# A second place for the sum of halves, rows' columns interleaved, a table loaded and cast later, and the last mixed sums of the first sequence in two halves

## The chip, the cores and the metric

One core of one Trainium2 chip runs the whole program in one launch. The metric is the device time in microseconds (us), the median of three runs. The traces come from one profiled execution of each kernel. Engines are named as the profile names them: PE (TensorE), DVE (VectorE), ACT (ScalarE), POOL (GpSimd), SP (SyncE, which here issues all loads and stores). Each engine works through its own instructions in a fixed order.

## The reference

There are eight sequences of 3136 rows with 256 columns. First a spectral layer, then a block with a two-dimensional transform and an MLP:

```
X  = rfft(x, axis=1);  Yr = Xr@w_r - Xi@w_i + b_r;  Yi = Xr@w_i + Xi@w_r + b_i
Y  = soft_threshold(Yr, 0.01) + 1j*soft_threshold(Yi, 0.01);  y = irfft(Y, n=3136)
u  = y + real(fft(fft(y, axis=1), axis=2))
un = (u - mean(u)) / sqrt(var(u) + 1e-6)
out = u + relu(un @ w_ch1) @ w_ch2
```

The weights are real-valued matrices of 256x256 (spectral) and 256x1024, 1024x256 (MLP).

## The kernel before

**Stages.** Transforms over 3136 are done as 64 x 49 with tables. For each sequence `b` there are ten generators: `p1` (64-point transform, result to DRAM in `aq` or `ad`), `p2_f2` (49-point transform of `af`, a load of that result, with the table `tff`), `p2_w` (weights, bias, threshold, giving `Y`), `p2_mix` (the two-dimensional transform's real part from `Y`, as sums and differences `mq`, stored to `md`), `p2_yt` and `p2_g2` (inverse 49-point transform with the table `tif`, result `bev` stored to `bd`), `p3_norm` (load `bf` from `bd` and `mt` from `md`, inverse 64-point transform, `ut` = the sum of both, row statistics and the scale `rs`), `p3_tr` (transposes of `ut`), `p3_mlp1` and `p3_mlp2`. Stages `p2_*` work in four quarters `q` of the frequencies, stages `p3_*` in 6 or 7 groups of up to 4 blocks of 128 rows (`z` blocks; 52 groups in all).

**Two numbers for one.** Most products are made with a high part and a rest, three matmuls each (`mm3`, L166): `uth` and `utl`, `hh` and `hl`, `tih` and `til`. The first sequence's transforms use plain fp32 instead.

**The order.** Every generator yields a due time (multiples of `T`, with shares like `TR`, `MLAG`, `NRM`) ahead of each step; a heap runs the steps by due time, and that is the priority with which the scheduler places the instructions on each engine at build time. `tc.issue_after(x)` and `behind(key, ...)` place an instruction behind another on the same engine. A tile is a named place (`tag`) with `bufs` copies: an instruction that writes a new tile waits until the last user of the place that it takes over is done.

**What the change touches.** `rows_f2` (L441) loads `af` into three places. In `p2_mix` (L557) the four products of a quarter come first and are then combined in one go (L608 to L616): on DVE for the first sequence, on POOL for the others, with copies on ACT; then the stores to `md` (L621 to L635). In `p2_yt` the table `tif` is loaded and for b > 0 cast to `tih` on ACT (L658), its rest `til` taken on DVE. In `p3_norm` the scales of a group are stored to a small DRAM tile `rd` (L737) as rows of 128. In `p3_tr` each pair of blocks, as soon as its `ut` is there, is transposed into one PSUM bank for both column halves `k` (L779), and evicted to `uth` (ACT, L781) and `utl` (DVE). `p3_mlp1` ends with the adds on POOL that form `total` from `uth` and `utl` (L806), in the one place `tot`:

```
total = sb.tile([128, 2, 512], F32, tag="tot", bufs=1, name="total")
...
gp.tensor_add(total[:, k, cols], uth[:, k, cols].bitcast(F32), utl[:, k, cols].bitcast(F32))
```

`p3_mlp2` loads the scales, spread over all partitions, as `rb` (L824) at step 1 of its 8, multiplies the result by it (L830), adds `total` (L833) and stores the sum from the `total` tile to the output (L834). `uth` and `utl` have two places each; a group's are free when its first MLP matrix and the adds of `total` are done. `ut` has four places. `split_double` uses `tot` once, early, for a part of the weights.

Of the kernel before, what the change touches and what calls it, by code (L numbers as in the profile page):

```python
# [20 lines left out]
D = 256  # L21
# [119 lines left out]
def spectral_block(ctx: ExitStack, tc: tile.TileContext, x, w_ri, b_ri, w1, w2,  # L141
# [30 lines left out]
    def split_double(name, h, l, parts, centred):  # L172
# [11 lines left out]
        if spare:  # L184
            pair = sb.tile([128, 2, 512], F32R, tag="tot", bufs=1, name="cv_pair")
        for sl, raw in parts:
# [240 lines left out]
    def clock2(b, q):  # L427
# [3 lines left out]
        return t0 + step * q, step, f2w, w0, ww, w0 + ww  # L431
    xt, yt_, tabs = {}, {}, {}

# [7 lines left out]
    def rows_f2(b, q, s):  # L441

        u0 = 8 * q
        af = sb.tile([98, 4 * D], F32, tag="af", bufs=3, name="af")
        ad, u = a_dram[b](u0 + 4 * s)
        ld = nc.sync.dma_start(out=af.rearrange("p (u d) -> p u d", d=D), in_=ad.rearrange("n r c u d -> (n r c) u d")[:98, u:u + 4])
        tff = sb.tile([98, 4, 100], F32, tag="tff", bufs=3, name="tff")
        nc.sync.dma_start(out=tff, in_=c_tf[:, u0 + 4 * s:u0 + 4 * s + 4, :])
        if b == 0:
            af_ld[2 * q + s] = ld.ins  # L450
            done.add(("af", 2 * q + s))
        return af, tff
# [53 lines left out]
    def p2_w(b):  # L506

        for q in range(4):
# [19 lines left out]
            for o in range(2):  # L528
                yield base + STEP * WW * o / 2
                gw = prod("wr", o, xs_[len(xs_) // 2:])  # L530
                ks = sb.tile([128, 8, S], F32, tag="ks", bufs=2, name="ks")
                sc.copy(ks, gw)
                for c in range(2):
# [12 lines left out]
    def p2_mix(b):  # L546
# [12 lines left out]
        for q in range(4):  # L559
# [24 lines left out]
            mq = sb.tile([100, 2, 4, 2, 128], F32, tag="mq", bufs=2, name="mq")  # L584
            even, odd = mq[:, 1, :, 0], mq[:, 1, :, 1]
            for ui in range(4):
# [19 lines left out]
                va.tensor_add(mq[:, 0, ui, 1, 0:1], gv[:, 0, 1, 0:1], odd[:, ui, 0:1])  # L606

            for i, f in ((0, va.tensor_add), (1, va.tensor_sub)):  # L608
                f(even[:, :, i::2], even[:, :, i::2], odd[:, :, 0:1].to_broadcast((100, 4, 64)))
            eng = gp if b else va  # L610
            eng.tensor_add(mq[:, 0, :, 0, 1:], even[:, :, 1:], odd[:, :, 1:])
            eng.tensor_sub(mq[:, 0, :, 1, 1:], even[:, :, 1:], odd[:, :, 1:])
            sc.copy(mq[:, 0, :, 0, 0:1], even[:, :, 0:1])
            sc.copy(even[:, :, 1:], mq[:, 0, :, 1, 1:])
            (va.tensor_copy if b else sc.copy)(odd[:, :, 1:], mq[:, 0, :, 0, 1:])
            sc.copy(odd[:, :, 0:1], mq[:, 0, :, 1, 0:1])  # L616
            mr = mq.rearrange("p a u h e -> p a (u h e)")
# [22 lines left out]
    def p2_yt(b):  # L640

        for q in range(4):
# [4 lines left out]
            for i in range(4):  # L647
                yield base + STEP * (M0 + 0.022 + 0.185 * i)
                s = i // 2
                if i % 2 == 0:  # L650
                    tif = sb.tile([100, 4, 98], F32, tag="tif", bufs=2, name="tif")
                    behind(3 if b or q else 1, out=tif, in_=c_ti[:, u0 + 4 * s:u0 + 4 * s + 4, :])
                    if b == 0:
                        tabs[b, q, s] = tif, None
                    else:
                        tih = sb.tile([100, 4, 98], F32R, tag="tih", bufs=1, name="tih")
                        til = sb.tile([100, 4, 98], F32R, tag="til", bufs=1, name="til")
                        sc.copy(tih, tif)  # L658
                        lo_v(til, tif, tih)
# [18 lines left out]
    def p2_g2(b):  # L678

        bd = b_dram[b] = dr.tile([NM, 2, 2, U, D], F32, tag="bd", bufs=4, name=f"bd{b}")  # L680
        for q in range(4):
            base, STEP, F2W, W0, WW, M0 = clock2(b, q)
            for i in range(4):
# [13 lines left out]
                u = 8 * q + 2 * i  # L697
                st_eng.dma_start(out=bd.rearrange("n r c u d -> (n r c) u d")[:98, u:u + 2], in_=bev.rearrange("p (u d) -> p u d", d=D))
        done.add(("b", b))
# [9 lines left out]
    def p3_norm(b):  # L709

        def finish(m, n, g, mt):
# [23 lines left out]
            if m + n == g0 + z:  # L735
                rd = scales[b, gi] = dr.tile([512], F32, tag="rd", bufs=4, name="rd")
                st_eng.dma_start(out=rd[:128 * z].rearrange("(j p) -> p j", j=z), in_=rall[:, :z].rearrange("p j o -> p (j o)"))  # L737
        for m, n in [(4 * i, 4) for i in range(6)] + [(NM - 1, 1)] * (b % 2):
# [26 lines left out]
    def p3_tr(b):  # L765
        for gi, (g0, z) in enumerate(GROUPS[b % 2]):
            t0, T3 = clock3(b, g0)
            for i, n in parts_of[z]:
                yield t0 + T3 * (TR + i / 4)
                if i == 0:  # L770
                    uth = sb.tile([128, 2, 512], F32R, tag="uth", bufs=UTHB, name="uth")
                    utl = sb.tile([128, 2, 512], F32R, tag="utl", bufs=2, name="utl")
                    uthl[b, gi] = uth, utl
                ut = uts.pop((b, g0 + i))
                g = gtile("g_ut")
                gv = g.rearrange("p (k t) -> p k t", k=2)
                for j in range(n):
                    for k in range(2):
                        te.transpose(gv[:, k, j * 128:(j + 1) * 128], ut[:, j, k * 128:(k + 1) * 128], ident)  # L779
                tw = slice(i * 128, i * 128 + n * 128)  # L780
                sc.copy(uth[:, :, tw], gv[:, :, :n * 128])  # L781
                lo_v(utl[:, :, tw], gv[:, :, :n * 128], uth[:, :, tw])

    def p3_mlp1(b):
        for gi, (g0, z) in enumerate(GROUPS[b % 2]):
# [15 lines left out]
            yield t0 + T3 * 1.0  # L801
            total = sb.tile([128, 2, 512], F32, tag="tot", bufs=1, name="total")
            for k in range(2):
# [5 lines left out]
    def p3_mlp2(b):  # L809
        for gi, (g0, z) in enumerate(GROUPS[b % 2]):  # L810
            t0, T3 = clock3(b, g0)
            w = z * 128
            for f in range(8):
# [5 lines left out]
                for k, o in enumerate(ops):  # L819
                    es = slice(k * 128, k * 128 + 128)  # L820
                    mm3(o, w2h[:, f, es], w2l[:, f, es], hh[:, :w], hl[:, :w], start=f == 0, stop=f == 7, first=1)
                if f == 1:
                    rb = sb.tile([128, 512], F32, tag="rb", bufs=1, name="rb")
# [107 lines left out]
```

## Time and profile before

| | before |
|---|---|
| median of 3 runs | 1941.72 us (1937.23 to 1942.70) |
| profiled execution | 1940.12 us, of which 1938.3 us from the first to the last instruction (span) |
| mean granted TensorE clock | 0.973 |
| busy: PE, DVE, ACT, POOL | 1841.4, 1192.2, 807.5, 560.4 us |

Busy time is the union of an engine's instructions. The granted clock is a share of 2.4 GHz; it has two levels, 0.5 (1.2 GHz) and 1, and a value between is a mean over the stretch. Line numbers (L806) are those of the kernel before.

### The profile page before, as it was taken

How to read it: one execution, taken by the hardware profiler on the slowest of the kernel's cores; microseconds unless marked ns; L12 is line 12 of the kernel's file. 1: busy time of each engine (PE TensorE's matmuls, PEld its weight loads, DVE VectorE, ACT ScalarE, POOL GpSimd, SP SyncE). 2: the span in 40 equal slices, each digit the busy share in tenths (PEclk: the TensorE clock that was granted, in tenths of full speed). 3: DMA queues.
4: the chain of work that ended last, by engine and by line, in shares of the span. 5: the costliest groups of instructions: out<-in, count | busy, mean ns of one | idle time of the engine just before them, and what ended most of it. 6: DMA issues, size and time to landing. Idle time of an engine off the chain costs nothing.

```text
span 1938.3 us, 29340 instructions
## 1 busy us (share of the span) xinstructions
PE 1841.4 (95%) x10044; PEld 1504.3 (78%) x10044; DVE 1192.2 (62%) x2603; ACT 807.5 (42%) x1864; POOL 560.4 (29%) x1028
## 2 busy tenths in 40 slices
PE   7886999899999999999999999999999999989998
PEld 4565787688787888877788788887878888867788
DVE  3664766566565766666666566656656656645543
ACT  2563544344444434444343444444444444322222
POOL 0003333222333422323323243332233433212121
PEclk8997999999999999999999999999999999999999
DMA  8763866455535756476444765546543543336211
GB/s 249 221 201 108 191 158 128 114 140 128 148 91 123 168 117 145 76 184 144 99 116 118 163 154 115 105 123 165 130 133 81 143 99 85 75 86 112 62 37 33
DMA packets 176365, 245.59 MB, mean 127 GB/s; under 512 B 42640, under 2 KB 123608, under 8 KB 175960
## 3 DMA queue, kind: packets, MB, share of 16 engines
q1 hardware_dynamic: 176216, 243.72, 52.3%
q8 instruction: 79, 1.29, 0.4%
q14 instruction: 70, 0.57, 0.1%
HBM read 140.79 MB, written 102.86 MB: 126 GB/s over the span
## 4 chain that ended last, share of the span: by engine, by line
PE 74%; DMA 12%; DVE 6%; POOL 3%; SPq 2%; issue 2%; ACT 2%; DVEq 0%; POOLq 0%; ACTq 0%
PE h L166 23%; PE o L166 23%; PE g_w L166 7%; PE g_f L477 4%; PE g_g L166 3%; DMA out_dram<-total 3%; PE g_g L377 2%; PE g_yt L665 2%; DMA mt<-md 2%; DMA bd<-bev 2%; PE g_ut L779 2%; PE g_f L377 2%; DMA xf<-in_x 2%; DMA md<-mq 1%; POOL total L806 1%
## 5 line engine op out<-in xcount | busy, mean ns | idle before, releaser
L799 DVE SCALAR_TENSOR_TENSOR hl<-h,hh 128x512 fp32r<-128x512 f32 (+2 forms) x416 | 273.1, 657 | 382.2 <-ACT hh L798 375.9
L798 ACT ACTIVATE hh<-h 128x512 fp32r<-128x512 f32 (+2 forms) x416 | 238.5, 574 | 417.3 <-PE h L166 396.5
L166 PE MATMUL o<-hl,w2h 128*128 128x512 f32 (+2 forms) x832 | 333.8, 401 | 9.9 <-DVE hl L799 7.6
L166 PE MATMUL h<-utl,w1h 128*128 128x512 f32 (+2 forms) x832 | 325.6, 391 | 2.8 <-DVE utl L156 2.8
L166 PE MATMUL h<-uth,w1l 128*128 128x512 f32 (+2 forms) x832 | 320.8, 386 | 0.0
L166 PE MATMUL h<-uth,w1h 128*128 128x512 f32 (+2 forms) x832 | 319.4, 384 | 0.0
L166 PE MATMUL o<-hh,w2l 128*128 128x512 f32 (+2 forms) x832 | 318.5, 383 | 0.0
L166 PE MATMUL o<-hh,w2h 128*128 128x512 f32 (+2 forms) x832 | 318.3, 383 | 0.0
L806 POOL TENSOR_TENSOR total<-uth,utl 128x256 f32<-128x256 f32 x200 | 146.4, 763 | 527.0 <-DMA out_dram<-total 404.2
L166 PEld LDWEIGHTS o<-hl,w2h 128*128 128x128 f32 x832 | 158.3, 190 | 47.1 <-DVE hl L799 13.5
L166 PEld LDWEIGHTS h<-utl,w1h 128*128 128x128 f32 x832 | 158.1, 190 | 35.8 <-issue 6.5
L166 PEld LDWEIGHTS h<-uth,w1l 128*128 128x128 f32 x832 | 158.2, 190 | 33.9 <-issue 4.1
L166 PEld LDWEIGHTS o<-hh,w2l 128*128 128x128 f32 x832 | 158.0, 190 | 29.7 <-issue 0.8
L166 PEld LDWEIGHTS h<-uth,w1h 128*128 128x128 f32 x832 | 158.3, 190 | 25.7
L166 PEld LDWEIGHTS o<-hh,w2h 128*128 128x128 f32 x832 | 158.6, 191 | 19.6
L477 PEld LDWEIGHTS g_f<-tff,af 98*128 98x128 f32 x1024 | 141.9, 200 | 32.5 <-DVE wdl L156 9.9
L477 PE MATMUL g_f<-tff,af 98*128 98x100 f32 x1024 | 150.3, 282 | 11.5 <-DMA af<-aq 9.1
L159 POOL TENSOR_TENSOR Xl<-xx,Xh 128x400 fp32r<-128x400 f32 x84 | 91.2, 1087 | 192.2 <-ACT Xh L494 188.9
L696 ACT COPY bev<-g_g 98x512 f32<-98x512 f32 x128 | 74.8, 585 | 113.9 <-PE g_g L166 59.2
L537 DVE SCALAR_TENSOR_TENSOR y<-g_w,bias,ks 128x400 f32<-128x400 f32 x128 | 80.5, 629 | 49.4 <-PE g_w L166 34.0
L540 POOL TENSOR_TENSOR Y<-y,m 128x400 f32<-128x400 f32 x56 | 62.5, 1117 | 166.5 <-DVE m L539 160.0
L665 PE MATMUL g_yt<-ident,Y 128*100 128x128 f32 x512 | 85.1, 281 | 24.5 <-POOL Y L544 7.8
(156 smaller groups left out, 3271.8 us busy)
## 6 DMA issues: line engine op xcount, KB each, us to landing
bd<-bev SPq DMA_DIRECT2D x128, 196.0 KB
bf<-bd SPq DMA_DIRECT2D x96, 256.0 KB
mt<-md SPq DMA_DIRECT2D x192, 128.0 KB
out_dram<-total SPq DMA_DIRECT2D x88, 256.0 KB
af<-ad SPq DMA_DIRECT2D x56, 392.0 KB
md<-mq SPq DMA_DIRECT2D x112, 192.0 KB
ad<-ev SPq DMA_DIRECT2D x84, 256.0 KB
xf<-in_x SPq DMA_DIRECT2D x39, 512.0 KB
```

What stands on the lines that cost most here:

```text
L159: gp.tensor_sub(out_, full, hi.bitcast(F32))
L166: te.matmul(o, l, r, start=start and i == 0, stop=stop and i == 2)
L377: return te.matmul(banks[i][64 * j:64 * j + 64], mat[rows, rows], movs[i][j], start=True, stop=True)
L477: te.matmul(gf[:, k, :, s], afs[s][:, ui * D + k * 128:ui * D + k * 128 + 128], tfs[s][:, ui].rearrange("p (c j) -> p c j", c=2), start=Tr ...
L537: va.scalar_tensor_tensor(y1, gw, bias[:, c, o:o + 1], ks, op0=ALU.add, op1=ALU.add)
L540: (va if b == 0 or o == 0 else gp).tensor_sub(y[:, o, :, c, :], y1, m)
L665: te.transpose(gt[:100, (v * 2 + o) * 128:(v * 2 + o + 1) * 128], y[:, o, place].rearrange("p c j -> p (c j)"), ident)
L696: sc.copy(bev, g[:98])
L779: te.transpose(gv[:, k, j * 128:(j + 1) * 128], ut[:, j, k * 128:(k + 1) * 128], ident)
L798: sc.activation(hh[:, :w], h[:, :w], AF.Relu)
L799: va.scalar_tensor_tensor(hl[:, :w], h[:, :w], 0.0, hh[:, :w].bitcast(F32), op0=ALU.max, op1=ALU.subtract)
L806: gp.tensor_add(total[:, k, cols], uth[:, k, cols].bitcast(F32), utl[:, k, cols].bitcast(F32))
```

## The change

There are six edits. (1) The place `tot` has two copies; `af` has two copies instead of three, and every third `af` of the first sequence takes `tot`. (2) In the last quarter of the first sequence the mixed sums are combined after every two of four blocks. (3) For the first quarter of the second sequence the table `tif` is loaded behind the last store to `bd`; for b > 0 the cast to `tih` stands behind the last copy `ks` of its quarter. (4) A group's columns stand in row order: row p of block j is column p*z + j, so that the scales are stored as 128 short rows of z numbers, the transposes write with a step of z, and the host reads the output back in that order. (5) `p3_tr` transposes all blocks of a group for column half 0, then for half 1, each into one bank. (6) `rb` is loaded at step 4 of 8.

```diff
@@ split_double, spectral_block, rows_f2 @@
-            pair = sb.tile([128, 2, 512], F32R, tag="tot", bufs=1, name="cv_pair")
+            pair = sb.tile([128, 2, 512], F32R, tag="tot", bufs=2, name="cv_pair")
...
-    xt, yt_, tabs = {}, {}, {}
+    xt, yt_, tabs, ks_in = {}, {}, {}, {}
...
-        af = sb.tile([98, 4 * D], F32, tag="af", bufs=3, name="af")
+        tag = "tot" if b == 0 and (2 * q + s) % 3 == 2 else "af"
+        af = sb.tile([98, 4 * D], F32, tag=tag, bufs=2, name="af")
@@ p2_w, p2_mix @@
-                sc.copy(ks, gw)
+                ks_in[b, q] = sc.copy(ks, gw).ins
...
-            even, odd = mq[:, 1, :, 0], mq[:, 1, :, 1]
+            odd = mq[:, 1, :, 1]
+
+            def combine(us):
+
+                even, odd = mq[:, 1, us, 0], mq[:, 1, us, 1]
+                for i, f in ((0, va.tensor_add), (1, va.tensor_sub)):
+                    f(even[:, :, i::2], even[:, :, i::2], odd[:, :, 0:1].to_broadcast((100, us.stop - us.start, 64)))
+                eng = gp if b else va
+                eng.tensor_add(mq[:, 0, us, 0, 1:], even[:, :, 1:], odd[:, :, 1:])
+                eng.tensor_sub(mq[:, 0, us, 1, 1:], even[:, :, 1:], odd[:, :, 1:])
+                sc.copy(mq[:, 0, us, 0, 0:1], even[:, :, 0:1])
+                sc.copy(even[:, :, 1:], mq[:, 0, us, 1, 1:])
+                (va.tensor_copy if b else sc.copy)(odd[:, :, 1:], mq[:, 0, us, 0, 1:])
+                sc.copy(odd[:, :, 0:1], mq[:, 0, us, 1, 0:1])
+            halves = b == 0 and q == 3
             for ui in range(4):
...
                 va.tensor_add(mq[:, 0, ui, 1, 0:1], gv[:, 0, 1, 0:1], odd[:, ui, 0:1])
-
-            for i, f in ((0, va.tensor_add), (1, va.tensor_sub)):
...
-            sc.copy(odd[:, :, 0:1], mq[:, 0, :, 1, 0:1])
+                if halves and ui % 2:
+                    combine(slice(ui - 1, ui + 1))
+            if not halves:
+                combine(slice(0, 4))
@@ p2_yt, p2_g2 @@
-                    behind(3 if b or q else 1, out=tif, in_=c_ti[:, u0 + 4 * s:u0 + 4 * s + 4, :])
+                    behind("bd" if b == 1 and q == 0 else 3 if b or q else 1, out=tif, in_=c_ti[:, u0 + 4 * s:u0 + 4 * s + 4, :])
...
-                        sc.copy(tih, tif)
+                        with tc.issue_after(ks_in[b, q]):
+                            sc.copy(tih, tif)
...
-                st_eng.dma_start(out=bd.rearrange("n r c u d -> (n r c) u d")[:98, u:u + 2], in_=bev.rearrange("p (u d) -> p u d", d=D))
+                stored = st_eng.dma_start(out=bd.rearrange("n r c u d -> (n r c) u d")[:98, u:u + 2], in_=bev.rearrange("p (u d) -> p u d", d=D))
+        af_ld["bd"] = stored.ins
         done.add(("b", b))
@@ p3_norm, p3_tr @@
-                st_eng.dma_start(out=rd[:128 * z].rearrange("(j p) -> p j", j=z), in_=rall[:, :z].rearrange("p j o -> p (j o)"))
+                st_eng.dma_start(out=rd[:128 * z].rearrange("(p j) -> p j", j=z), in_=rall[:, :z].rearrange("p j o -> p (j o)"))
...
-            for i, n in parts_of[z]:
-                yield t0 + T3 * (TR + i / 4)
-                if i == 0:
+            w = z * 128
+            for k in range(2):
+                yield t0 + T3 * (TR + k / 4)
+                if k == 0:
...
-                ut = uts.pop((b, g0 + i))
+                    blocks = [(uts[b, g0 + i], j) for i, n in parts_of[z] for j in range(n)]
                 g = gtile("g_ut")
-                gv = g.rearrange("p (k t) -> p k t", k=2)
-                for j in range(n):
-                    for k in range(2):
-                        te.transpose(gv[:, k, j * 128:(j + 1) * 128], ut[:, j, k * 128:(k + 1) * 128], ident)
-                tw = slice(i * 128, i * 128 + n * 128)
-                sc.copy(uth[:, :, tw], gv[:, :, :n * 128])
-                lo_v(utl[:, :, tw], gv[:, :, :n * 128], uth[:, :, tw])
+                gv = g[:, :w].rearrange("p (t j) -> p j t", j=z)
+                for i, (ut, j) in enumerate(blocks):
+                    te.transpose(gv[:, i], ut[:, j, k * 128:(k + 1) * 128], ident)
+                sc.copy(uth[:, k, :w], g[:, :w])
+                lo_v(utl[:, k, :w], g[:, :w], uth[:, k, :w])
@@ p3_mlp1, p3_mlp2 @@
-            total = sb.tile([128, 2, 512], F32, tag="tot", bufs=1, name="total")
+            total = sb.tile([128, 2, 512], F32, tag="tot", bufs=2, name="total")
...
-                if f == 1:
+                if f == 4:
                     rb = sb.tile([128, 512], F32, tag="rb", bufs=1, name="rb")
```

On POOL, in the second sequence's second quarter (`y_1718` and `y_1766` before, `y_1724` and `y_1779` after, are the two subtractions L540 that make its `Y`; `vv`, `rs` the norm of a group). Before:

```order
L732 TENSOR_SCALAR vv<-vv 128x2
L733 TENSOR_TENSOR rs<-rs,vv 128x2
L540 TENSOR_TENSOR Y<-y_1718,m 128x8x50
L540 TENSOR_TENSOR Y<-y_1766,m 128x8x50
L159 TENSOR_TENSOR Xl<-xx,Xh 128x4x100
```

After:

```order
L743 TENSOR_SCALAR vv<-vv 128x2
L744 TENSOR_TENSOR rs<-rs,vv 128x2
L816 TENSOR_TENSOR total<-uth,utl 128x256 x2
L541 TENSOR_TENSOR Y<-y_1724,m 128x8x50
L816 TENSOR_TENSOR total<-uth,utl 128x256 x2
L541 TENSOR_TENSOR Y<-y_1779,m 128x8x50
L159 TENSOR_TENSOR Xl<-xx,Xh 128x4x100
```

The four adds of the second group now stand around these subtractions; before, they came twenty rows later, ahead of the next quarter's.

On SP, at the end of the first sequence's sums (`md` stores, `bf` and `mt` loads of its first norm groups). Before:

```order
L748 DMA bf<-bd_87 128x2x256 x2
L282 DMA tif<-c_ti 100x392
L621 DMA md_86<-mq 24x2x1024
L622 DMA md_86<-mq 2x1x1024
L623 DMA md_86<-mq 24x2x1024
L633 DMA md_86<-mq 24x2x1024
L634 DMA md_86<-mq 2x1x1024
L635 DMA md_86<-mq 24x2x1024
L446 DMA af<-ad_85 98x1024
L448 DMA tff<-c_tf 98x400
L748 DMA bf<-bd_87 128x2x256 x2
L753 DMA mt<-md_86 32x4x256
```

After:

```order
L449 DMA tff<-c_tf 98x400
L630 DMA md_86<-mq 24x2x1024
L631 DMA md_86<-mq 2x1x1024
L632 DMA md_86<-mq 24x2x1024
L642 DMA md_86<-mq 24x2x1024
L643 DMA md_86<-mq 2x1x1024
L644 DMA md_86<-mq 24x2x1024
L759 DMA bf<-bd_87 128x2x256 x2
L449 DMA tff<-c_tf 98x400
L764 DMA mt<-md_86 32x4x256
```

The second `bf` pair and the `tif` load now follow the `md` stores, and only two pairs instead of three stand ahead of the first `mt` load.

On PE, between the first two sets of transposes (`g_w`, `g_f`, `g_yt` belong to the second sequence, `h` is the first MLP product). Before:

```order
L166 MATMUL g_w<-Xh,wdl 128x400
L665 MATMUL g_yt<-ident,Y 100x128
L477 MATMUL g_f_1398<-tff,af 128x2x50 x4
L477 MATMUL g_f_1411<-tff,af 128x2x50 x4
L665 MATMUL g_yt<-ident,Y 100x128
L477 MATMUL g_f_1433<-tff,af 128x2x50 x4
L779 MATMUL g_ut<-ident,ut 128x128 x4
L166 MATMUL h<-utl,w1h 128x512
```

After:

```order
L166 MATMUL g_w<-Xh,wdl 128x400
L166 MATMUL h<-utl,w1h 128x512
L166 MATMUL h<-uth,w1h 128x512
L166 MATMUL h<-uth,w1l 128x512
L166 MATMUL h<-utl,w1h 128x512
L166 MATMUL h<-uth,w1h 128x512
L166 MATMUL h<-uth,w1l 128x512
L675 MATMUL g_yt<-ident,Y 100x128
L790 MATMUL g_ut<-ident,ut 128x128 x4
```

Six matmuls of `h`, those of column half 0, now stand ahead of the second four transposes.

## Rows read from the trace of the kernel before

**Rows 1.** The page: busy time of PE (share of the span, instructions) and the engines behind it, the packets of all DMA queues, and the chain that ended last by engine.

```profile
PE 1841.4 (95%) x10044; PEld 1504.3 (78%) x10044; DVE 1192.2 (62%) x2603; ACT 807.5 (42%) x1864; POOL 560.4 (29%) x1028
DMA packets 176365, 245.59 MB, mean 127 GB/s; under 512 B 42640, under 2 KB 123608, under 8 KB 175960
PE 74%; DMA 12%; DVE 6%; POOL 3%; SPq 2%; issue 2%; ACT 2%; DVEq 0%; POOLq 0%; ACTq 0%
```

**Rows 2.** Busy time by stretches: start:end and length in us, then for PE, PEld, DVE, ACT and POOL the busy us and (x) the instructions, the granted clock, the share that the DMA engines were busy, GB/s.

```profile
0.00:128.00 128.00, 105.87 (x456) 66.35 (x456) 75.72 (x170) 55.67 (x121) 0.41 (x6) 0.91 0.75 230
128.00:182.00 54.00, 34.09 (x178) 28.57 (x177) 23.87 (x56) 23.53 (x57) 18.40 (x27) 0.78 0.54 153
155.00:160.00 5.00, 1.48 (x9) 1.15 (x7) 1.17 (x3) 0.49 (x1) 0.00 (x0) 0.92 1.00 256
328.00:341.00 13.00, 8.37 (x39) 7.14 (x38) 4.75 (x11) 5.09 (x11) 5.51 (x8) 0.74 0.62 194
369.00:382.00 13.00, 5.55 (x26) 4.65 (x25) 2.51 (x6) 3.38 (x8) 3.52 (x6) 0.74 0.93 293
950.00:960.00 10.00, 7.46 (x32) 5.46 (x32) 5.35 (x7) 4.13 (x10) 6.30 (x8) 0.83 0.32 110
1406.00:1416.00 10.00, 7.89 (x44) 5.74 (x36) 4.56 (x6) 2.55 (x6) 6.36 (x7) 0.83 0.12 41
1558.00:1570.00 12.00, 7.77 (x48) 7.52 (x47) 5.86 (x15) 3.53 (x12) 6.65 (x6) 0.72 0.17 47
```

**Rows 3.** The line L806 by itself: the adds' durations in ns (least, median, most) with the first and last start in us, and one of the releasers for which POOL sat idle before them (us, times).

```profile
L806 POOL TENSOR_TENSOR total<-uth,utl x200: 450/745/1213, 168.3 to 1924.5; 128x256 f32<-128x256 f32 x100
  DMA out_dram<-total: 404.2, 38
```

**Rows 4.** Timeline of PE in eight stretches: start and duration in us, instruction, count, and in brackets the idle time before it and what ended it.

```profile
335.31 0.51 PE L166 MATMUL g_g<-yl,tih 100*98 100x256 f32 x1 [4.63 <-DVE Xl L156]
378.06 0.88 PE L665 MATMUL g_yt<-ident,Y 128*100 128x128 f32 x3 [7.45 <-POOL Y L544]
492.06 0.53 PE L665 MATMUL g_yt<-ident,Y 128*100 128x128 f32 x3 [2.41 <-POOL Y L540]
843.62 0.50 PE L166 MATMUL o<-hl,w2h 128*128 128x512 f32 x1 [1.26 <-DVE hl L799]
953.38 0.53 PE L665 MATMUL g_yt<-ident,Y 128*100 128x128 f32 x3 [2.46 <-POOL Y L540]
1304.37 0.50 PE L166 MATMUL o<-hl,w2h 128*128 128x512 f32 x1 [1.17 <-DVE hl L799]
1411.00 0.53 PE L665 MATMUL g_yt<-ident,Y 128*100 128x128 f32 x3 [2.10 <-POOL Y L540]
1564.01 0.58 PE L166 MATMUL o<-hl,w2h 128*128 128x256 f32 x1 [4.23 <-DVE hl L799]
```

**Rows 5.** The chain of work that ended last, in order of time, of the whole execution: start, duration, what. Five of its longest pieces.

```profile
318.25 11.52 DMA out_dram<-total
369.53 5.54 DMA out_dram<-total
604.37 12.87 DMA xf<-in_x
831.92 4.92 DMA rb<-rd
865.84 11.56 DMA bd<-bev
```

**Rows 6.** Timeline from 95 to 180 us of DVE, ACT, SP (SPq: the issue alone) and PE, columns as in rows 4.

```profile
143.69 1.51 DVE L612 TENSOR_TENSOR mq<-mq 100x508 f32<-100x508 f32 x1
145.24 0.61 ACT L614 COPY mq<-mq 100x508 f32<-100x508 f32 x1 [0.34 <-DVE mq L612]
145.87 0.89 SPq L748 DMA_DIRECT2D bf<-bd  x2
147.30 0.54 SPq L621 DMA_DIRECT2D md<-mq  x1
164.88 1.29 DVE L714 TENSOR_TENSOR ut<-g_g,mt 128x512 f32<-128x512 f32 x2 [8.68 <-DMA mt<-md]
165.72 1.09 PE L779 MATMUL g_ut<-ident,ut 128*128 128x128 f32 x4 [9.24 <-DVE ut L714]
176.36 0.80 PE L166 MATMUL h<-utl,w1h 128*128 128x512 f32 x1 [2.81 <-DVE utl L156]
```

**Rows 7.** Groups by line and shape: count, busy us, mean ns of one, idle us before them.

```profile
L779 PE MATMUL g_ut<-ident,ut 128*128 128x128 f32 x392 | 61.1, 279 | 10.4 <-DVE ut L714 10.4
```

**Rows 8.** Timeline of PE from 1012 us, at the full clock: one set of transposes and the matmuls of `o` behind it.

```profile
1013.00 0.60 PE L779 MATMUL g_ut<-ident,ut 128*128 128x128 f32 x4
1013.67 0.39 PE L166 MATMUL o<-hh,w2h 128*128 128x512 f32 x1
1013.90 0.39 PE L166 MATMUL o<-hh,w2l 128*128 128x512 f32 x1
```

**Rows 9.** Timeline of SP and PE: a load of `af`, and its first reader's matmuls.

```profile
792.71 0.33 SPq L446 DMA_DIRECT2D af<-ad  x1
833.10 1.48 PE L477 MATMUL g_f<-tff,af 98*128 98x100 f32 x12
```

More of the change, by code (lines that the diff above doesn't have):

```diff
@@ L606, in p2_mix @@
                 va.tensor_add(mq[:, 0, ui, 1, 0:1], gv[:, 0, 1, 0:1], odd[:, ui, 0:1])
-            for i, f in ((0, va.tensor_add), (1, va.tensor_sub)):
[L609 to L615, printed above, removed]
-            sc.copy(odd[:, :, 0:1], mq[:, 0, :, 1, 0:1])
+                if halves and ui % 2:
+                    combine(slice(ui - 1, ui + 1))
+            if not halves:
+                combine(slice(0, 4))
             mr = mq.rearrange("p a u h e -> p a (u h e)")
@@ L918 @@
             at = s * (NM - 1) + g0
-            y[:, :, at:at + z] = raw[:, :, at * D:(at + z) * D].reshape(nb // 2, 128, 2, z, 128).transpose(0, 4, 3, 2, 1)
+            y[:, :, at:at + z] = raw[:, :, at * D:(at + z) * D].reshape(nb // 2, 128, 2, 128, z).transpose(0, 3, 4, 2, 1)
     y = y.reshape(nb // 2, 2, 2, 32, N2, D)
```

## The prediction

> **What bounds the kernel now.** The head of the page comes first [rows 1]: PE is busy for 95% of the span, DVE for 62%, ACT 42%, POOL 29%, and the chain that ended last is 74% PE. So only time in which PE stands still or runs at its lower clock can be saved, unless PE's own work changes. The table by stretches sizes it [rows 2]: 1938.0 us less 1841.4 us busy leaves 96.6 us idle. The first 128 us hold 22 us of that and the stretch 128 to 182 us another 20; there the first sequence hands over to its norm and MLP. After that the idle time sits in short holes; around the larger ones the granted clock is 0.72 to 0.83.
>
> Next, who ends those holes. For the adds that form `total` (POOL, L806), POOL idles 404 us in 38 waits for a landing of `out_dram<-total` [rows 3]. Most of that costs nothing, as POOL is 29% busy. But POOL works in order, and at eight places PE's wait ends at something that stood behind such an add [rows 4]. The chain of waits shows one link by link [rows 5]: the store issued at 369.53 lands after 5.54 us, POOL can start the adds, and PE goes on at 378.06, when they and a memset of Y behind them are done; it idled 7.45 us. The cause is the single `tot` place: the adds of group g wait until the store of group g-1 has landed, and that store follows the end of that group's second MLP matrix.
>
> **The change, part by part.** The sum is made against the profiled execution's own 1940.1 us (span 1938.3 and 1.8 around it); the median shown, 1941.7, is 0.1% above it, which I neglect.
>
> *Second place for `total`.* The adds of group g now wait for the store of group g-2. There are 52 groups and the first adds start at 168 us [rows 3], so one comes every (1938 - 168) / 52 = 34 us; the longest store of [rows 5] took 11.52 us. A store that has a whole group more to land is not waited for. The order agrees: on POOL the adds move ahead of the subtractions of a quarter that they used to follow by some twenty rows (shown above). Idle removed [rows 4]: 4.63 + 7.45 + 2.41 + 1.26 + 2.46 + 1.17 + 2.10 + 4.23 = 25.7 us. Around five of them the granted clock was low [rows 2]. With a share (1 - clock)/0.5 of the stretch at 1.2 GHz and half of PE's busy time there lost, 328:341 gives 0.52 x 8.37 / 2 = 2.2 us, 369:382 gives 1.4, 950:960 and 1406:1416 give 1.3 each, 1558:1570 gives 2.2: 8.4 us. Ends: 0 and 34.1 us (no loss: a place more is never waited for longer). I take 29, near the upper end, since the store is all that the chain names ahead of the adds [rows 5]; 5 us I leave to whatever comes late next.
>
> *The first handover (combine in halves, inverse table later).* PE waits until 165.72 for `ut`, that for `mt<-md`, and that for the last stores of the mixed sums, issued from 147.30 on [rows 6]. The first two blocks are now combined before the last two are multiplied, so half of each operation from L609 to L616 is left at the end: half of 1.51 us on DVE and of two copies of 0.61 us on ACT, 1.4 us. SP can use that: in the new order (shown above) the six `md` stores stand ahead of the second `bf` pair, issued from 145.87, and of a `tif` load, and 147.30 becomes some 145.9. Ahead of the first `mt` loads there are now two `bf` loads of 256 KB and one `tif` of 153 KB less, 0.66 MB; the DMA engines were full there, 1.00 busy at 256 GB/s [rows 2], so 2.6 us. The halves add a few short instructions to DVE and ACT, which idle here (8.68 us on DVE before `ut`, [rows 6]); they cost nothing, or under 1 us if that cover were gone. The cast of the inverse table, now behind the copy `ks`, takes a wait for a load off ACT and a subtraction off DVE in the middle of this chain; that is in the 1.4 us. Sum 4.0 us, ends 0 and the 9.24 us hole.
>
> *Transposes by column half.* The first transposes now need both `ut` of a group instead of one. At the first handover both adds take 1.29 us [rows 6], so about 0.6 us is lost once; elsewhere four places of `ut` cover it. In return the first matmuls of `h` need only column half 0; PE's order now puts six of them ahead of the second transposes, where before all waited 2.81 us for the second eviction [rows 6]. I count 2 us gained, and 1 us of clock: the handover together 4.0 - 0.6 + 2 + 1 = 6.4 us, taken as 6.
>
> *Columns in row order.* The price here is a write with a step of `z` elements (16 bytes where z is 4) into PSUM, which no row shows with such a step. The count is 392 transposes [rows 7]. One lasts 0.28 us [rows 7], and at the full clock four take 0.60 us [rows 8], so one starts every 0.11 us with 128 columns: 0.84 ns a column. Matmuls of `o` with 512 columns start every 0.23 us [rows 8]: 0.45 ns a column into the same memory. So the transposes deliver columns at about half the rate that PSUM takes in line, and a step that costs up to this factor is hidden. Ends: 0 (a step can't speed a write up), and 392 x 0.11 = 43 us if every transpose takes twice its time. I take 0, the end that the nearest row speaks for; the 43 us stay for the range.
> The Trainium skill, SBUF — State Buffer, section "Door 1: The DMA port swizzle", says in its note on cachelines that PSUM has lines of 8 bytes and that a non-contiguous PSUM access pattern slows matmuls significantly. It speaks against this edit; no row here shows it, and by it the sum would be the second rival below.
>
> *The scale's store and load.* The store of `rd` goes from 44 x 512 + 4 x 384 + 4 x 256 = 25,088 pieces of 4 bytes (of the 42,640 packets under 512 B in [rows 1]) to 52 x 128 = 6,656 of up to 16. Nobody on the path waits for it: 0. The load of `rb` moves from step 1 to step 4 of 8; three steps of a 34 us group are 12.8 us, and in the chain it took 4.92 us [rows 5]. Cost 0; were it later, DVE would wait at L830 and hold the `o` banks. It also takes a load that waits for DVE out of SP's way, which I do not price.
>
> *`af` from three places to two.* A load now waits for the quarter before. That happened already: the load at 792.71 follows the last `g_f` of a quarter and its first reader starts at 833.10 [rows 9], 40 us later. Cost 0; in the first sequence `tot` lends the third place, and SP's order is the same up to the loads of the second sequence.
>
> *The order.* All engines' orders are drawn anew. The other holes, 96.6 - 22 - 20 - 26 = 29 us, are small and spread out. They can shrink or grow; I allow 3 us of loss, between -6 and +10.
>
> Sum: 1940.1 - 29 - 6 + 3 = **1908 us**, 1.7% less. Best case 34 + 11 + 6 = 51 less, 1889. The likeliest case's own range is 1889 to 1924.
>
> **Rivals.**
> *Next wait (0.15).* The store is no longer waited for, but its place is taken: by `bd` and `xf` transfers, which land after 11.56 and 12.87 us in the same chain [rows 5] and share one queue with all others. For it: a busy DMA at both big holes (0.62 and 0.93 in [rows 2]); against it: the last three have 0.12 to 0.32. Half of the 34 us comes back: 1940 - 17 - 4 + 6 = 1925.
> *Stepped writes cost (0.13), the one that ends slower.* Place: L779, on PE, which has no cover. The gain above is 32 us, so the sign turns at 32 / 392 = 0.082 us more per transpose; at twice the time (0.11 more) it is 1908 + 43 = 1951, with three times 1994. For it: no two columns then lie side by side; against it: the slack of 0.84 to 0.45 ns [rows 8]. What the page named above states is this rival; its "significantly" has no size in it.
> *It does not do what it says (0.08).* The store goes out so late on SP, which waits in order for DVE, that the second place is in use as well when the adds come due: POOL's wait stays, and only the handover gains, 1934 to 1942.
>
> **How the numbers follow.** The forecast has 0.64. About 0.3% (6 us) is what a measurement of this kernel can tell from no change: faster is under 1936, slower over 1947. Forecast 0.64 and 0.13 of the first rival are faster: 0.77. The rest of that rival, 0.06 of the third and 0.03 of the second (a smaller price, 25 to 40 us) are no change: 0.11. Slower are 0.10 of the second and 0.02 of the third: 0.12. The range has to take in the first rival and the third: 1889 to 1942; outside are the costly writes and a little at the low end.
>
> **What would show it.** Right: POOL's idle time before the `total` adds ended by `out_dram` falls from 404 us to under 100; none of the eight holes has POOL behind that store; PE's idle sum falls from 97 us to about 65; `g_ut` keeps its 0.11 us step; `ut` starts before 162 us. Wrong: a step of `g_ut` over 0.15 us, or a PE idle sum above 85 us with other releasers, `mt` or `bev`, in the place of POOL.

## The result and the profile after

The change takes 1865.94 us (median of 4 runs, 1863.14 to 1866.78) against 1939.47 us for the kernel before on the same chip: 0.9619 of it, 95% interval 0.9596 to 0.9643. The forecast was 1908 us in a range of 1889 to 1942: the sign was right, but the change gained 73 us where 32 were forecast. The profiled execution took 1863.14 us, with a span of 1861.3 us.

The head of the page and its chain, as in [rows 1], and between them the queue that carries nearly all transfers (packets, MB, and the time of its packets as a share of 16 engines' span):

```profile
PE 1811.1 (97%) x10044; PEld 1486.1 (80%) x10044; DVE 1190.9 (64%) x2611; ACT 808.4 (43%) x1872; POOL 556.3 (30%) x1028
DMA packets 157932, 245.58 MB, mean 132 GB/s; under 512 B 24208, under 2 KB 105176, under 8 KB 157528
q1 hardware_dynamic: 157784, 243.72, 44.9%
PE 89%; DVE 4%; DMA 3%; SPq 1%; ACT 1%; POOL 1%; issue 1%; DVEq 0%; ACTq 0%; POOLq 0%
```

PE's idle time is 1861.3 - 1811.1 = 50.2 us where it was 96.9: 46.7 us gone. PE's busy time fell by 30.3 us as well, for the same 10044 matmuls. Transfers are no longer 12% of the chain but 3%. Of the queue, the page of before says this:

```profile
q1 hardware_dynamic: 176216, 243.72, 52.3%
```

The same 243.72 MB took 52.3% of 16 x 1938.3 us before, 16,220 us of packet time, and 44.9% of 16 x 1861.3 us after, 13,370 us. The same bytes in 18% less packet time were in no term of the prediction. Little of it is the small pieces' own time. Worked out from the packets of both traces, those of up to 16 bytes took 454 us before and 232 after; the rest is in the 132,552 packets of 1 to 4 KB, the same number in both, which took 118 ns each (mean) before and 98 ns after.

Busy time by stretches (columns as in [rows 2]), first before, then after:

```profile
190.00:400.00 210.00, 196.47 (x1105) 159.79 (x1104) 132.73 (x290) 95.23 (x224) 67.72 (x113) 0.95 0.61 143
400.00:1000.00 600.00, 586.13 (x3280) 484.64 (x3279) 386.56 (x840) 261.21 (x608) 192.76 (x345) 0.99 0.57 132
1000.00:1600.00 600.00, 585.31 (x3358) 492.71 (x3358) 392.24 (x863) 266.87 (x629) 205.42 (x361) 0.99 0.54 125
```

```profile
190.00:400.00 210.00, 206.82 (x1186) 170.06 (x1185) 149.51 (x308) 98.96 (x231) 73.73 (x121) 1.00 0.51 150
400.00:1000.00 600.00, 599.78 (x3404) 497.34 (x3404) 396.81 (x874) 274.09 (x639) 203.81 (x365) 1.00 0.46 133
1000.00:1600.00 600.00, 599.78 (x3473) 507.89 (x3472) 398.96 (x889) 273.97 (x642) 205.02 (x365) 1.00 0.44 128
```

In 1200 us in the middle PE idled 28.6 us before and 0.4 us after, and the granted clock is 1.00 where it was 0.99. So not only the eight holes of [rows 4] closed: the small ones that the prediction left alone closed too. In the same stretches the DMA engines are busy for 0.46 and 0.44 of the time where it was 0.57 and 0.54, and move as much per second.

The adds that form `total`, their durations and releasers, as in [rows 3]:

```profile
L816 POOL TENSOR_TENSOR total<-uth,utl x200: 457/745/1163, 163.6 to 1834.6; 128x256 f32<-128x256 f32 x100
  DMA out_dram<-total: 300.3, 34
```

POOL still waits for the landing of `out_dram`, 300 us in 34 waits where the prediction wanted under 100. That wait just no longer reaches PE. The chain's transfers behind the handover (start, duration, what), to be read against [rows 5]:

```profile
589.68 1.77 DMA bd<-bev
1033.33 1.79 DMA bd<-bev
1654.82 2.67 DMA bf<-bd
1661.06 4.04 DMA md<-mq
1667.13 3.37 DMA mt<-md
```

Pieces of 11 to 13 us are gone. For three of the five in [rows 5], one and the same store had stood one row ahead. The timeline of SP in the kernel before (start, duration of the issue, what), at 317, 603 and 864 us:

```profile
317.77 0.39 SPq L737 DMA_DIRECT2D rd<-rs  x1
318.25 0.45 SPq L834 DMA_DIRECT2D out_dram<-total  x1
...
603.90 0.36 SPq L737 DMA_DIRECT2D rd<-rs  x1
604.37 0.43 SPq L282 DMA_DIRECT2D xf<-in_x  x1
...
864.99 0.38 SPq L737 DMA_DIRECT2D rd<-rs  x1
865.84 0.31 SPq L698 DMA_DIRECT2D bd<-bev  x1
```

Each of the three long transfers, a different tensor each time, was issued 0.5 to 0.9 us behind the scale store `rd`. The whole chain has eight pieces over 10 us: seven start 0.5 to 1.9 us behind such a store, and 2.4 us into the eighth one is issued. For a full group that store moves 2 KB, in 512 pieces of 4 bytes. It starts no chain piece itself, which is why the prediction gave it nothing.

The handover and the transposes answer to [rows 6], [rows 7] and [rows 8]: PE and DVE in the first handover, the group of the transposes, and two of them at the full clock.

```profile
148.15 1.99 PE L377 MATMUL g_g<-bf,inv_f 64*64 64x512 f32 x8 [8.06 <-DMA bf<-bd]
157.56 1.29 DVE L725 TENSOR_TENSOR ut<-g_g,mt 128x512 f32<-128x512 f32 x2 [14.77 <-DMA mt<-md]
158.31 0.45 PE L166 MATMUL g_w<-Xsh,wrh 128*128 128x400 f32 x1 [2.93 <-DVE ut L725]
163.54 0.50 PE L166 MATMUL h<-utl,w1h 128*128 128x512 f32 x1 [1.24 <-DVE utl L156]
```

```profile
L790 PE MATMUL g_ut<-ident,ut 128*128 128x128 f32 x392 | 60.1, 273 | 1.0 <-DVE ut L725 1.0
```

```profile
1005.08 0.38 PE L790 MATMUL g_ut<-ident,ut 128*128 128x128 f32 x2
```

The wait that `ut` ends is 2.93 us instead of 9.24 (it now stands before a `g_w`, as the order of PE is another), and the first `h` starts at 163.54 instead of 176.36. But PE waits 8.06 us for the first `bf`, where the kernel before waited 5.29; from 128 to 182 us it idles 17.5 us where it was 19.9, with 212 matmuls instead of 178. Of the stepped transposes, two take 0.38 us: one of 0.27 and a step of 0.11, as before.

### The profile page after: what moved, and what is told of

Read it like the earlier page. It is cut to its first block, busy times and chain, and to the rows that moved or that the text cites. A ratio compares the mean times of both kernels' runs of the same rounds, so it can differ in the third digit from the quotient of the medians.

```text
span 1861.3 us, 29330 instructions
## 1 busy us (share of the span) xinstructions
PE 1811.1 (97%) x10044; PEld 1486.1 (80%) x10044; DVE 1190.9 (64%) x2611; ACT 808.4 (43%) x1872; POOL 556.3 (30%) x1028
## 3 DMA queue, kind: packets, MB, share of 16 engines
q1 hardware_dynamic: 157784, 243.72, 44.9%
## 4 chain that ended last, share of the span: by engine, by line
PE 89%; DVE 4%; DMA 3%; SPq 1%; ACT 1%; POOL 1%; issue 1%; DVEq 0%; ACTq 0%; POOLq 0%
PE o L166 29%; PE h L166 28%; PE g_w L166 9%; PE g_f L478 5%; PE g_g L166 4%; PE g_yt L675 3%; PE g_g L377 2%; PE g_ut L790 2%; PE g_f L377 2%; PE g_mix L612 2%; PE g_w L524 1%; PE g_mix L614 1%; DMA raw_w<-in_w 1%; DMA md<-mq 1%; DMA bf<-bd 0%
## 5 line engine op out<-in xcount | busy, mean ns | idle before, releaser
L478 PEld LDWEIGHTS g_f<-tff,af 98*128 98x128 f32 x1024 | 140.7, 198 | 28.6 <-DVE wdl L156 9.5
L738 POOL TENSOR_SCALAR vv<-ag 128x2 f32<-128x2 f32 (+1 forms) x100 | 22.7, 227 | 243.8 <-DVE ag L735 229.5
```

The costliest lines, as they stand in the source:

```text
L478: te.matmul(gf[:, k, :, s], afs[s][:, ui * D + k * 128:ui * D + k * 128 + 128], tfs[s][:, ui].rearrange("p (c j) -> p c j", c=2), start=Tr ...
```

## The experiments

Two theories stood at the start of the runs. **Theory P** (the prediction's): the second place for `total` takes POOL's waits away, and so PE's holes. **Theory S**: the short pieces of the scale store slow every transfer near them, and row order takes that away. Each kernel was timed against the kernel before on the same chip; the medians of before were 1939.28 us for a1 to b2, 1937.64 for c1 to c4, 1939.80 for d1 to d4, 1940.07 for e1 to e4.

### One edit put in, one taken out

a1 is the kernel before with the second place alone:

```
-            pair = sb.tile(..., tag="tot", bufs=1, name="cv_pair")
+            pair = sb.tile(..., tag="tot", bufs=2, name="cv_pair")
-        af = sb.tile([98, 4 * D], F32, tag="af", bufs=3, name="af")
+        tag = "tot" if b == 0 and (2 * q + s) % 3 == 2 else "af"
+        af = sb.tile([98, 4 * D], F32, tag=tag, bufs=2, name="af")
-            total = sb.tile([128, 2, 512], F32, tag="tot", bufs=1, name="total")
+            total = sb.tile([128, 2, 512], F32, tag="tot", bufs=2, name="total")
```

> The kernel before with the second place for the sums alone (edit 1, with the places of af that pay for it). Theory P (place): the store that the adds on POOL wait for was behind nearly all late holes of PE, the small ones too; 1940 falls to 1875 to 1890. Theory S (short pieces): the scale's stores in pieces of 4 bytes kept the DMA queue busy and made all other transfers land late; the place alone takes away only the eight holes that were counted, 1905 to 1915, and rd<-rs still lands some 10 us after its issue.

a2 is the kernel before with the store's row order alone, and b2 the change with the old order put back:

```
-  st_eng.dma_start(out=rd[:128 * z].rearrange("(j p) -> p j", j=z), in_=...)
+  st_eng.dma_start(out=rd[:128 * z].rearrange("(p j) -> p j", j=z), in_=...)
```

> The kernel before with one line changed: a group's scales go to DRAM in rows of z numbers (as in the change), and nothing else; the scales then meet the wrong columns, so the numbers put out differ. The order of all engines is the same as before. Theory P: nobody on the path waits for this store, 1936 to 1942. Theory S: packets of 1 to 4 KB take 20 to 30% less time, as they do after the change, out_dram lands in some 3 us instead of 5, and the time falls to 1885 to 1905.

> The changed kernel with one line undone: the scales go to DRAM in pieces of 4 bytes again, as rows of 128 (they then meet the wrong columns). The order of all engines stays that of the changed kernel. Theory P: 1864 to 1870. Theory S: packets take as long as before the change, small holes come back at bd, mt and ut, 1885 to 1905.

b1 is the change without a1's edit (`tot` with one place, `af` with three).

> The changed kernel without edit 1 (one place for the sums, three for af). Theory P: the holes come back, 1915 to 1930. Theory S: stores land early, and most of the gain stays, 1870 to 1890.

Measured: a1 1928.47 us (0.9946, interval 0.9928 to 0.9964), a2 1872.06 (0.9657, 0.9632 to 0.9681), b1 1870.70 (0.9647, 0.9625 to 0.9669), b2 1902.37 (0.9813, 0.9786 to 0.9840). Theory P falls and Theory S holds: one line of the store, with the order of every engine unchanged, gives 67 of the 73 us, and the second place 11 us alone and at most 5 in the change, where the intervals of b1 and after overlap. Theory S's figures missed: 1885 to 1905 us was too little gain for a2, and 1905 to 1915 too much for a1.

The same two stores in the traces, with the same list of issues around them. First before, from 4 us ahead of the store at 561.50, then a2 around 542.03; a digit and a number are 0.5 us, busy tenths of the DMA engines and GB/s, then the queue in these 20 us:

```profile
DMA  6868575889776986999678956897894788762000
GB/s 131 172 180 180 164 254 156 274 225 270 242 215 173 185 57 53 86 127 123 135 118 174 144 146 121 144 164 140 211 158 110 239 265 304 274 261 107 16 0 0
q1 hardware_dynamic: 1980, 3.23, 77.0%
```

```profile
DMA  7678676789765993988888998830000795300000
GB/s 172 131 172 213 123 270 189 242 250 266 267 223 140 194 98 37 119 135 184 299 344 330 378 367 312 246 109 26 0 0 0 193 261 172 122 0 0 0 0 0
q1 hardware_dynamic: 1606, 3.27, 59.7%
```

Before, the engines stay busy and move 53 to 211 GB/s for 8 us; in a2 they reach 299 GB/s 6 us earlier after the store than before reaches 239, and the burst ends 5 us sooner. The fall right behind the store itself, to 37 GB/s in a2, is short. The place is not an exception: over all 52 stores, in the time from 2 to 10 us behind the issue, the DMA engines move 62 GB/s at 0.61 busy before and 133 GB/s at 0.46 in a2 (worked out from the packets of the traces).

### What a second place does to the wait

a1's trace says why the place brought so little. Releasers of POOL ahead of the adds in a1, as in [rows 3]:

```profile
  DMA out_dram<-total: 407.1, 37
```

With two places POOL waits as long as with one (404.2 us in 38). Worked out over the 52 groups, the first add of a group comes 5.1 us (median) behind the issue of the previous group's second store before; in a1 it comes 5.1 us behind that of the group before the previous one. From a group's adds to its second store it was 28 us, and is 64. The order moved the adds forward by one group, and the new place was full again. So most of PE's holes stayed: in the 1200 us in the middle PE idles 23.9 us in a1 where it was 28.6. PE's waits that `Y` from POOL and `hl` from DVE ended (us in total, times, longest), first before, then a1, then a2:

```profile
PE g_yt L665 <- POOL Y L544: 7.8, 2, 7.4
PE g_yt L665 <- POOL Y L540: 7.0, 3, 2.5
PE o L166 <- DVE hl L799: 7.6, 6, 4.2
```

```profile
PE g_yt L666 <- POOL Y L545: 5.8, 2, 4.9
PE g_yt L666 <- POOL Y L541: 5.6, 3, 2.1
PE o L166 <- DVE hl L800: 13.4, 7, 4.2
```

```profile
PE g_yt L665 <- POOL Y L544: 1.8, 2, 1.1
PE o L166 <- DVE hl L799: 0.8, 4, 0.3
```

With one place and the other store, a2 has hardly any of them left. POOL's wait in the kernel after, one of the 34, first SP, then POOL:

```profile
792.57 0.46 SPq L844 DMA_DIRECT2D out_dram<-total  x1
```

```profile
797.47 1.44 POOL L816 TENSOR_TENSOR total<-uth,utl 128x256 f32<-128x256 f32 x2 [3.63 <-DMA out_dram<-total]
```

### The other edits alone, in the kernel before

c3 has the handover edits alone (the sums in halves, `tif` behind `bd`, its cast behind `ks`), c4 the load of `rb` at `f == 4` instead of `f == 1`, d1 the transposes by channel halves with contiguous columns; all three keep the 4-byte store. The core of d1:

```
-            for i, n in parts_of[z]:
+            for k in range(2):
...
+                gv = g[:, :w].rearrange("p (j t) -> p j t", j=z)
+                for i, (ut, j) in enumerate(blocks):
+                    te.transpose(gv[:, i], ut[:, j, k * 128:(k + 1) * 128], ident)
```

> The kernel before with the handover edits alone: the last mixed sums of the first sequence in two halves, and the second sequence's inverse table loaded behind the last store of the first and cast behind ks. The 4-byte store stays. The prediction counted 6 us for the handover as a whole, so 1933 us (1928 to 1940). The change with the 4-byte store put back lies 26 us below a1; if the handover is what gives those 26 us, this kernel lies at 1910 to 1920 us.

> The kernel before with the load of the scales moved from the second to the fifth of the eight steps of the second product, nothing else. The prediction gave this 0, so 1939 us (1934 to 1944). If the load of the scales, waiting in SP's queue for the store in 4-byte pieces, holds back the loads behind it, it gives part of the 26 us that a1 and the change with the 4-byte store differ by: 1915 to 1930 us.

> The kernel before with the transposes of the third stage split by halves of the channel (all blocks' first halves, then all second halves, with casts of one half each), columns in PSUM contiguous as before, the 4-byte store as before. What b2's 37 us leave after a1's 11 and c3's 7 is 19 us. If the split gives it, 1919 us (1912 to 1926). The prediction gave the split nothing by itself: 1938 us (1930 to 1946).

Measured: c3 1930.44 us (0.9962, 0.9944 to 0.9980), c4 1937.39 (0.9995, 0.9978 to 1.0013), d1 1912.74 (0.9848, 0.9803 to 0.9892). The handover edits give 7 us, where the prediction had 4.0 for these alone and 6 with the split and a share of clock. The load gives nothing. The split gives 27 us: the prediction had 2 less 0.6 for it, and the 19 us left of b2's 37 would be 1919 us in a range of 1912 to 1926, at whose end 1912.74 lies. Yet these gains are not the change's. With the row-order store, all edits but the second place are a2 to b1: 1872.06 to 1870.70, no difference that can be told. And alone they give 11 + 7 + 27 = 45 us where together, in b2, they give 37. A reading that fits, and that no run shows by itself, is that they move work away from late transfers, and that nothing is left to gain when these are no longer late. Which wait d1 shortened isn't settled: its order differs from before's on every engine.

### The stepped writes

d2 is the change with contiguous columns in PSUM, every engine's order as after:

```
-                gv = g[:, :w].rearrange("p (t j) -> p j t", j=z)
+                gv = g[:, :w].rearrange("p (j t) -> p j t", j=z)
```

> The kernel after with contiguous columns in PSUM for the transposes instead of steps of 16 bytes, the short-row store kept (the scales then meet their columns in another order, so those products are other numbers); every engine's order is that of after. If the stepped writes cost nothing, 1866 us (1862 to 1870). The rival of the prediction, stepped writes that slow the transposes, gives less: from 1823 us, where its whole upper price of 43 us is paid, to 1860.

Measured: 1865.89 us against 1865.94 for after, and the 392 transposes are busy for 60.2 us in d2 and 60.1 in after. Writing with steps of 16 bytes costs them nothing that can be told. The Trainium skill (SBUF — State Buffer, section "Door 1: The DMA port swizzle") says that a non-contiguous PSUM pattern slows matmuls significantly; for 128-column transposes of f32 this pair of runs doesn't show it.

### What of the pieces costs

Five kernels (d3, d4, e1, e3, e4) add a store per group to the change, behind the first, into DRAM that nobody reads, so that no instruction waits for it; c1 and c2 change the one store of the kernel before (in the 44 groups of four blocks; the other 8 keep theirs).

```
 c1  for a in range(2): st_eng.dma_start(out=rd.rearrange("(p c a) -> p c a", a=2, c=2)[:, :, a], in_=...)
 c2  st_eng.dma_start(out=rd.rearrange("(c p a) -> p c a", c=2, a=2), in_=...)
 d3  st_eng.dma_start(out=more[:128 * z].rearrange("(j p) -> p j", j=z), in_=rall[:, :z]...)
 d4  st_eng.dma_start(out=more[:128 * z].rearrange("(p j) -> p j", j=z), in_=rall[:, :z]...)
 e1  st_eng.dma_start(out=more[:256].rearrange("(j p) -> p j", j=2), in_=rall[:, :2]...)
 e3  ...out=more[:128 * z * 16].rearrange("(j p s) -> p j s", j=z, s=16)[:, :, 0], in_=rall[:, :z]...
 e4  ...out=more[:512 * z].rearrange("(r p j) -> p r j", r=4, j=z), in_=(the z sums, four times)
```

> The kernel before, with the scale store of the groups of four blocks split in two: each puts 256 pieces of 4 bytes at steps of 8 bytes, so that a partition's four sums still lie side by side in DRAM, but arrive as 512 pieces of 4 bytes, as many and as small as before. (As in a2, the scales then meet their columns in row order, so those products are other numbers.) Theory Count: the number of pieces slows the other transfers, wherever they land; then the time stays that of before, 1939 us (1930 to 1946). Theory Neighbours: it is pieces of different partitions next to each other in DRAM; then it is near a2's 1872 us (1866 to 1885).

> The kernel before, with the scale store of the groups of four blocks in 256 pieces of 8 bytes, two sums of a partition side by side, the partitions next to each other, and the second pair of sums behind the 128 first. Theory Count: half the pieces cost about half of the 67 us, so 1905 us (1893 to 1920). Theory Neighbours: pieces of different partitions still lie next to each other, so most of the cost stays, 1925 to 1942 us.

> The kernel after with a second scale store per group behind the first, in 512 pieces of 4 bytes, into a DRAM tile that nobody reads. No instruction waits for it. If the small pieces slow the other transfers, it costs about what b2 costs without any wait on the store, 1890 to 1905 us. If it was the wait of the load of the scales for its store that cost b2 its 36 us, 1866 us (1862 to 1872).

> The same second store per group into a tile that nobody reads, but in row order, 128 pieces of 16 bytes: the price of one more store issue and its transfer. By either theory 1866 to 1870 us; if a second store costs as much in this form, what d3 shows is the price of a store and not that of its pieces.

> As d3, the kernel after with an extra store that nobody reads, but half of the pieces, 256 of 4 bytes (the sums of two of the four blocks). d3's 512 cost 43 to 46 us over d4 and after. If the cost goes with the number, 1889 us (1882 to 1896); if a store of small pieces costs as such, as d3, 1911 us; if only a long row of them hurts, near 1868 us.

> As d3, 512 extra pieces of 4 bytes, but each 64 bytes from the next in DRAM, so that no two lie side by side. Theory Neighbours: it is pieces next to each other that collide, so this costs little, 1866 to 1880 us. Theory Count or Size: as d3, 1911 us (1903 to 1918).

> As d3, 512 extra pieces, but of 16 bytes (each partition's four sums written four times, to four places). Theory Size: pieces of 16 bytes are harmless, as the 128 of d4 were, so 1866 to 1875 us. Theory Count: 512 pieces cost what they cost at 4 bytes, 1911 us (1903 to 1918). c2's 256 pieces of 8 bytes cost 17 us over a2 where 512 of 4 cost 66, so something between is open too.

| kernel | pieces of a full group | bytes each | next piece | us | ratio to before [95%] | cost |
|---|---|---|---|---|---|---|
| before | 512 | 4 | adjoining | 1937.6 to 1940.1 | 1 | 67 over a2 |
| c1 | 2 x 256 | 4 | 8 bytes on | 1918.68 | 0.9892 [0.9860, 0.9924] | 47 over a2 |
| c2 | 256 | 8 | adjoining | 1888.66 | 0.9742 [0.9712, 0.9771] | 17 over a2 |
| a2 | 128 | 16 | adjoining | 1872.06 | 0.9657 [0.9632, 0.9681] | 0 |
| d3 | 512 | 4 | adjoining | 1911.51 | 0.9847 [0.9789, 0.9905] | 46 over after |
| e1 | 256 | 4 | adjoining | 1882.69 | 0.9707 [0.9688, 0.9726] | 17 over after |
| e3 | 512 | 4 | 64 bytes on | 1866.97 | 0.9627 [0.9611, 0.9643] | 1 over after |
| e4 | 512 | 16 | adjoining | 1868.32 | 0.9630 [0.9611, 0.9650] | 2 over after |
| d4 | 128 | 16 | adjoining | 1868.19 | 0.9622 [0.9587, 0.9658] | 2 over after |

c1 and c2 came out at neither of their two expectations. c1 shows that row order as such isn't what helps: with 4-byte pieces it keeps 47 of the 67 us. Some 4 of c2's 17 us belong to the 8 groups that keep their old store (an estimate: 256 or 384 pieces each, at the price per store that e1 and d3 give). d3 settles that the cost isn't a wait for the store: nobody waits for it, and it costs 46 us. d4 settles that it isn't the price of one more store. e3 is the surprise: as many pieces, as small, but 64 bytes apart, cost nothing. So neither the number nor the size alone does it: many small pieces that lie close together in DRAM do. They need not adjoin within one store, as c1's, 8 bytes on (the second store fills the gaps), cost 47 us; and with 16 bytes a piece they may adjoin. e3 changes two things at once, the distance and the stretch of DRAM that a store covers (32 KB instead of 2); which of them counts, and what distance between 8 and 64 bytes is enough, no run separates. The head lines of d3 and of e3, same number of packets and bytes:

```profile
DMA packets 183853, 245.69 MB, mean 129 GB/s; under 512 B 50128, under 2 KB 131096, under 8 KB 183448
q1 hardware_dynamic: 183704, 243.83, 53.6%
```

```profile
DMA packets 183853, 245.69 MB, mean 132 GB/s; under 512 B 50128, under 2 KB 131096, under 8 KB 183448
q1 hardware_dynamic: 183704, 243.83, 46.1%
```

The same place in both, 20 us from 842.5 in d3 and from 825.4 in e3, the extra store being issued 4.0 us in:

```profile
DMA  9863989999999999989959589879622100000000
GB/s 203 57 74 115 328 332 379 385 416 375 280 199 186 132 134 99 100 119 104 103 89 66 76 119 127 137 224 320 234 90 82 57 29 0 0 0 0 0 0 0
```

```profile
DMA  9988899999899799997543004700000000000000
GB/s 289 213 197 277 291 363 393 387 387 299 185 247 179 221 326 322 300 234 172 135 127 123 8 0 135 242 25 0 0 0 0 0 0 0 0 0 0 0 0 0
```

In d3 the engines are mostly 8 or 9 tenths busy while they move 66 to 137 GB/s for 6.5 us, and the burst around the store ends 5 us later than in e3. Over all 52 extra stores, from 2 to 10 us behind the issue, it is 56 GB/s at 0.60 busy in d3 and 123 GB/s at 0.45 in e3 (worked out as above). Why close pieces slow the other transfers, inside the memory path, no run here shows.

## Why the prediction was wrong

**The step that failed** is the term of the scale's store: "Nobody on the path waits for it: 0." The premise held as far as the runs show (the later load of the scales gives nothing in c4). The conclusion was wrong: d3's extra store, which nobody waits for, costs 46 us. What the term measured is a gain of 67 us alone (a2) and 36 in the change (b2 less after). A transfer was priced by who waits for it, not by what it does to the transfers beside it. The rows said more: the prediction counted 25,088 pieces, and quoted chain pieces of 11.52, 12.87 and 11.56 us [rows 5] without asking why 196 to 512 KB took that long. It read them as a busy queue, the first rival, and the range got no bound for the term on the side of a gain.
The Trainium skill (DMA: Bandwidth & Descriptors) says in its section "Specifications" that below 512 bytes a transfer is read, modified and written, and in "Rules for kernel authors" that a strided last dimension should be rearranged to be contiguous. The second rule is the edit that paid (67 us in a2). The first doesn't separate e3 and d4, whose pieces are under 512 bytes too and cost 1 and 2 us, from d3.

**Second place for `total`**: taken at 29 us, measured 11 alone and at most 5 in the change. The step "a store that has a whole group more to land is not waited for" failed too: the prediction saw the adds move forward in the new order and read it as agreement, but that move is what used the place up (407 us of waiting in a1, where it was 404). The eight holes did close in the change, but they close with one place too: of the 1200 us in the middle PE idles 2.3 us in b1 and 1.7 in a2. What made them was that landings were late, not that there was one place. What the third rival said of POOL's wait came true (300 us in 34 waits), because the adds moved forward, and without harm.

**The handover**: its own edits, at 4.0 us of the 6, measured 7 in the kernel before; in the change they aren't told apart from nothing, though the wait that `ut` ends fell from 9.24 to 2.93 us. **The split by halves**, counted there at 2 us less 0.6, gave 27 us with the slow store: an interaction that the sum had no place for.

**Stepped writes** at 0, **the load of `rb`** at 0: right (d2, c4). **`af` in two places** at 0 was run only with the second place (a1 has both, b1 neither), which shows no loss. **The order**, 3 us of loss: none seen.

**The signs named**: a PE idle sum near 65 us is 50; the `g_ut` step held; `ut` came at 157.56, before 162 us; POOL's wait under 100 us did not come. None of these signs was about a transfer's own time, so none would have named the cause.

**Where the time went**: the two profiled spans differ by 77.0 us, 46.7 of idle time and 30.3 of PE's busy time. Of the latter some 26 us are an estimate for matmuls at the lower of the two clocks: half of PE's busy time in the stretches of that clock, summed, is 38.5 us before and 12.3 after. The stretch 190 to 400 had a granted clock of 0.95 and 1105 matmuls, and has 1.00 and 1186.

## What to carry to other kernels

Price a small transfer twice: by who waits for it, and by what the transfers issued in the next microseconds do; a transfer of 196 to 512 KB that takes 12 us in the chain deserves the question of what was issued just ahead of it. Store columns of small values so that each partition writes at least 16 bytes in one piece, or keep the pieces apart (64 bytes were enough here). Add what edits give alone only where they don't shelter the same late work.

## What was not expected of the hardware

512 pieces of 4 bytes that adjoin in DRAM, 2 KB in all, left the DMA engines mostly 8 or 9 tenths busy at 66 to 137 GB/s for 6.5 us at the place shown; the 52 stores of a run, 44 of them of this size, cost 46 us (d3) to 67 us (a2). As many pieces 64 bytes apart cost 1 us (e3), 512 adjoining pieces of 16 bytes 2 us (e4). Half the pieces cost 17 us (e1), under half; so did 256 of 8 bytes (c2). Transposes that write PSUM with a step of 16 bytes start every 0.11 us, as without the step, and the time is that of d2.
